# The 0/1 matrix of a token's place is made once per column, and the token's number is multiplied into the narrow matrix

## The chip, the cores and the metric

One core of one Trainium2 chip runs the whole program in one launch. The metric is the device time of that core in microseconds (us), the median of several runs.

## The reference

Attention over pooled keys and values gives 4,608 tokens of 512 numbers. Each goes through one of 8 experts of a first layer, and then, where a skip score is positive, through one of 8 experts of a second one.

```python
def _attn_ref(q, k, v):                       # q, k, v: 8, 8, 576, 64
    k_p = k.reshape(B, H, Sp, pool, D).mean(axis=3)      # pool = 8
    v_p = v.reshape(B, H, Sp, pool, D).mean(axis=3)
    scores = scale * np.matmul(q, k_p.transpose(0, 1, 3, 2))
    ...
    return np.matmul(attn, v_p)

def _moe_ref(x, modality_id, w_gate, modality_bias, w1, w2):
    logits = x @ w_gate + modality_bias[modality_id]
    e_idx = np.argmax(logits, axis=1)
    ...
    for e in range(E):                        # E = 8, w1 512 x 1024, w2 1024 x 512
        mask = e_idx == e
        h = np.maximum(x[mask] @ w1[e], 0.0)
        out[mask] = gate_w[mask, None] * (h @ w2[e])

def _moe2_ref(x, w_skip, w_gate, w1, w2):
    do_compute = x @ w_skip > 0
    ...                                       # the same layer on x[do_compute], without bias
    out[do_compute] = xc + y
```

## The kernel before

**Three stages.** The attention works through 36 columns of 128 tokens. A MoE layer works through blocks of 256 tokens of one expert. In a block `gemm1` (L1300) makes 8 slices of the hidden layer by 12 products of 256 columns each, and `gemm2` (L1314) makes two halves (128 tokens each) of the output by 24 products of 512 columns each; every product stands three times, since numbers are split in a high and a low part. After a slice of `gemm1`, ScalarE makes `hh` (L1303) and VectorE makes `hl` (L1304), which frees the slice's PSUM bank. GpSimd gathers the rows of a block by an indirect DMA (L1245), and TensorE transposes them (L1265, `xT`).

**Where a token goes.** `route` gives for every token its expert, its place within a group of 128 places (`BB`), and which group it is (`RH`). `route_places` (L859) makes for each column of 128 tokens a matrix `OB`: a row for each token, a column for each of the 128 places, a one where the token has that place, times the token's number. The number is held in two parts, `pay`, so that bf16 holds each exactly; so there are two matrices for a column. The narrow matrix `oa` (L960 early, L1096 later) has a one where the token belongs to a group. The product of `OB`, transposed, with `oa`, summed over the columns (L975, L1104), gives for every slot the two parts of its token's number in `W`; `slot_rows` (L992, L994, L997) reads `W` and makes the indices of the gather.

**When.** For the first blocks of either layer, `early_places` and `early_slots` do this for two or four groups, before all tokens are known. For all later blocks `route_slots` does it for 52 groups, in steps of six columns, with the products three steps behind; that happens during block 1 of the layer (`second`, L1563), 36 columns in layer 1 and 52 in layer 2. In layer 2's routing, which runs within the blocks of layer 1, `route_places` makes two columns a block on GpSimd.

**What sets the order.** Nothing is scheduled by a program: instructions stand on each engine in the order in which the code issues them. The side work is written as generators. `bg.tick()`, called at fixed places of the main work, takes the next `bg.pace` steps of the first generator in the queue; `bg.flush()` takes all that are left. So the number of `yield`s decides beside which main work a step stands. In `second`, `tick` is called twice after each slice of `gemm1`, `flush` after the first half of `gemm2`, and then come `gather(2)` and, within the second half of `gemm2`, `xT(2)`.

## Time and profile before

| what | before |
|---|---|
| three runs | 1021.94, 1027.18, 1029.12 us, median 1027.18 |
| span of the profiled execution | 1021.7 us |
| mean granted clock of TensorE | 0.972 |
| TensorE busy | 953.3 us, 93% |
| VectorE busy | 713.9 us, 70% |
| GpSimd busy | 606.4 us, 59% |

The page has no time of the profiled execution beside its span, which runs from the first instruction to the last. It is 0.2 us under the fastest run and 5.5 us under the median. The shares are means over stages of different kinds: attention to about 200 us, block 0 and 1 of layer 1 to 275 us, steady blocks of layer 1 to about 750 us, layer 2 to the end.

### The profile page before, as it was taken

To read this page: it belongs to the slowest core of one execution; us is meant where nothing else is said; L and a number is where in the kernel's file an instruction comes from. 1 tells how busy PE (TensorE), PEld (TensorE's weight loads), DVE (VectorE), ACT (ScalarE), POOL (GpSimd) and SP (SyncE) were. 2 spreads that over 40 slices of the span, in tenths; PEclk is the share of its full clock that TensorE was granted. 3 is DMA by queue.
4 is the path that set the end of the run, shared out by engine and by line. 5 is a ranking of instruction groups with operands and counts; after the bars stand their busy time and mean duration, and the time that the engine had idled before them with its cause. 6 is when DMAs were issued, how large, how long until landed. Compare 5 with 4: busy or idle time off the path is not lost. (4 is left out here: it accounts for less than half of the span.)

```text
span 1021.7 us, 20008 instructions
## 1 busy us (share of the span) xinstructions
PE 953.3 (93%) x6647; PEld 859.1 (84%) x6647; DVE 713.9 (70%) x1683; ACT 526.0 (51%) x1072; POOL 606.4 (59%) x816
## 2 busy tenths in 40 slices
PE   6888879899999999999999999999898999999995
PEld 5787879787788888888888888888786998888995
DVE  6699998886666666666666766667455667667665
ACT  4345545432455555555555655555313556555454
POOL 4675856554577777677777777767544333444442
PEclk8789989998999999999999999999899999999998
DMA  9998864520111111342223511226214662661341
GB/s 226 205 248 245 199 172 156 177 68 9 43 53 68 56 60 57 126 148 69 71 73 118 170 68 62 70 71 206 93 56 132 217 226 83 204 207 33 103 154 31
DMA packets 88353, 123.51 MB, mean 121 GB/s; under 512 B 15615, under 2 KB 52479, under 8 KB 88224
## 3 DMA queue, kind: packets, MB, share of 16 engines
q1 hardware_dynamic: 77904, 94.38, 30.9%
q0 software_dynamic: 10320, 27.59, 8.6%
q8 instruction: 59, 0.97, 0.4%
q14 instruction: 70, 0.57, 0.2%
HBM read 181.29 MB, written 39.48 MB: 216 GB/s over the span
## 5 line engine op out<-in xcount | busy, mean ns | idle before, releaser
L1300 PE MATMUL ps_g<-xh,w1h 128*128 128x256 f32 x992 | 289.2, 291 | 13.2 <-DVE hl L1304 8.0
L1300 PE MATMUL ps_g<-xl,w1h 128*128 128x256 f32 x992 | 280.2, 283 | 0.0
L1300 PE MATMUL ps_g<-xh,w1l 128*128 128x256 f32 x992 | 280.2, 282 | 0.0
L1253 POOL TENSOR_TENSOR w1l<-w1r,w1h 128x512 fp32r<-128x512 f32 x122 | 156.6, 1305 | 150.9 <-ACT w1h L1252 150.1
L1303 ACT ACTIVATE hh<-ps_g 128x256 fp32r<-128x256 f32 x248 | 95.5, 385 | 231.4 <-PE ps_g L1300 225.8
L1300 PEld LDWEIGHTS ps_g<-xh,w1h 128*128 128x128 f32 x992 | 188.2, 190 | 22.1 <-DVE hl L1304 10.5
L1314 PE MATMUL ps_g<-w2h,hh 128*128 128x512 f32 x464 | 190.5, 411 | 0.6 <-DVE rs_v L994 0.5
L1300 PEld LDWEIGHTS ps_g<-xl,w1h 128*128 128x128 f32 x992 | 188.6, 190 | 0.6 <-DVE xl L1269 0.2
L1300 PEld LDWEIGHTS ps_g<-xh,w1l 128*128 128x128 f32 x992 | 188.2, 190 | 0.0
L1314 PE MATMUL ps_g<-w2h,hl 128*128 128x512 f32 x464 | 185.1, 399 | 0.0
L1314 PE MATMUL ps_g<-w2l,hh 128*128 128x512 f32 x464 | 185.0, 399 | 0.0
L1259 DVE TENSOR_TENSOR w2l<-w2r,w2h 128x512 fp32r<-128x512 f32 x227 | 162.9, 719 | 17.7 <-ACT w2h L1258 1.5
L1304 DVE SCALAR_TENSOR_TENSOR hl<-ps_g,hh 128x256 fp32r<-128x256 f32 x248 | 105.0, 423 | 91.4 <-ACT hh L1303 85.9
L1258 ACT CAST w2h<-w2r 128x512 fp32r<-128x512 f32 x232 | 141.8, 612 | 3.0 <-DVE gidxf L997 3.0
L1252 ACT CAST w1h<-w1r 128x512 fp32r<-128x512 f32 x240 | 135.4, 618 | 4.9 <-DMA w1r<-in_moe_w_dram 4.9
L859 POOL TENSOR_SCALAR OB<-iota,BB,pay 128x128 bf16<-128x128 bf16 x126 | 110.8, 888 | 24.7 <-DVE BB L847 24.7
L1314 PEld LDWEIGHTS ps_g<-w2h,hl 128*128 128x128 f32 x464 | 88.3, 190 | 20.8
L1253 DVE TENSOR_TENSOR w1l<-w1r,w1h 128x512 fp32r<-128x512 f32 x118 | 101.2, 880 | 5.6 <-POOL rt_eq L796 5.2
L1314 PEld LDWEIGHTS ps_g<-w2h,hh 128*128 128x128 f32 x464 | 88.5, 191 | 18.1 <-issue 1.5
L1314 PEld LDWEIGHTS ps_g<-w2l,hh 128*128 128x128 f32 x464 | 88.6, 191 | 16.8
L1269 DVE TENSOR_TENSOR xl<-ps_x,xh 128x512 fp32r<-128x512 f32 x64 | 43.8, 686 | 57.3 <-ACT xh L1268 57.3
L1373 ACT ACTIVATE x<-ps_g,gate 128x512 f32<-128x512 f32 x37 | 25.5, 689 | 82.4 <-PE R L831 43.4
(256 smaller groups left out, 1463.9 us busy)
## 6 DMA issues: line engine op xcount, KB each, us to landing
w1r<-in_moe_w_dram SPq DMA_DIRECT2D x128, 512.0 KB
w2r<-in_moe_w_dram SPq DMA_DIRECT2D x128, 512.0 KB
x2s<-x SPq DMA_DIRECT2D x19, 522.0 KB
v<-in_v_dram SPq DMA_DIRECT2D x16, 576.0 KB
xd<-x SPq DMA_DIRECT2D x16, 520.0 KB
q_sb<-in_q_dram SPq DMA_DIRECT2D x16, 512.0 KB
kt<-in_k_dram SPq DMA_DIRECT2D x8, 576.0 KB
x2s<-OBx SPq DMA_DIRECT2D x16, 261.0 KB
```

The source lines that it names most:

```text
L859: e.tensor_scalar(g.ob(c)[:, i, :], g.iota, r.BB[:, c:c + 1], r.pay[:, i, c:c + 1], ALU.is_equal, ALU.mult)
L1252: self.nc.scalar.copy(self.w1h[f], raw)
L1253: (eng or self.nc.vector).tensor_tensor(self.w1l[f], raw, self.w1h[f].bitcast(F32), ALU.subtract)
L1258: self.nc.scalar.copy(self.w2h[f], raw)
L1259: (eng or self.nc.vector).tensor_tensor(self.w2l[f], raw, self.w2h[f].bitcast(F32), ALU.subtract)
L1269: nc.vector.tensor_tensor(self.xl[i % 2][:, :, 128 * t:128 * t + 128], ps, hi.bitcast(F32), ALU.subtract)
L1300: nc.tensor.matmul(ps, lhsT=a[f][:, k, :], rhs=b[:, k, :], start=(n == 0), stop=(n == 11))
L1303: nc.scalar.activation(out=self.hh[f], in_=ps, func=ACTF.Relu)
L1304: nc.vector.scalar_tensor_tensor(self.hl[f], in0=ps, scalar=0.0, in1=self.hh[f].bitcast(F32), op0=ALU.max, op1=ALU.subtract)
L1314: nc.tensor.matmul(ps, lhsT=a[f][:, tt], rhs=b[f], start=(n == 0), stop=(n == 23))
L1373: nc.scalar.activation(out=self.x2[i % 2][:, t, 0:DM], in_=ps, func=ACTF.Copy, scale=self.gate[i % 2][:, t:t + 1])
```

## The change

`OB` gets one matrix per column, ones and zeros alone, and is made by one instruction in place of two. The token's number goes into `oa`: a new function multiplies the 0/1 matrix `eq` of the groups by either part of `pay` and puts the two results side by side, so that one product with twice as many columns takes the place of two. `route_places` now has one step for a column. Where the second engine helps (columns 18 to 26 and 27 to 35), it takes the odd columns. The buffer `OBx`, which `zero` clears, has half the size.

```diff
-    g.OB = [const.tile([128, C1, 2, 128], BF16, name="OB")]
+    g.OB = [const.tile([128, C1, 128], BF16, name="OB")]
...
 def route_places(tc, g, r, c0, n, eng, eng2=None):
     for c in range(c0, c0 + n):
-        for i in range(2):
-            if c > c0:
-                yield
-            e = eng2 if eng2 is not None and i else eng
-            e.tensor_scalar(g.ob(c)[:, i, :], g.iota, r.BB[:, c:c + 1],
-                            r.pay[:, i, c:c + 1], ALU.is_equal, ALU.mult)
+        e = eng2 if eng2 is not None and c % 2 else eng
+        e.tensor_scalar(g.ob(c), g.iota, r.BB[:, c:c + 1], None, ALU.is_equal)
         yield
+
+
+def places_tokens(tc, oa, eq, pay):
+
+    n, w = eq.shape[1], eq.shape[2]
+    for i in range(2):
+        tc.nc.vector.tensor_tensor(oa[:, :, i, :], eq,
+                                   pay[:, i, :].unsqueeze(2).to_broadcast([128, n, w]), ALU.mult)
...
-    oa = r.oa[C] = sp.tile([128, C, n], BF16, tag=f"er_oa{C}", name="er_oa", bufs=1)
-    V.tensor_tensor(oa, g.iota_a[:, j0:j0 + n].unsqueeze(1).to_broadcast([128, C, n]),
+    oa = r.oa[C] = sp.tile([128, C, 2, n], BF16, tag=f"er_oa{C}", name="er_oa", bufs=1)
+    eq = sp.tile([128, C, n], F32, tag=f"er_eq{C}", name="er_eq", bufs=1)
+    V.tensor_tensor(eq, g.iota_a[:, j0:j0 + n].unsqueeze(1).to_broadcast([128, C, n]),
                     a.unsqueeze(2).to_broadcast([128, C, n]), ALU.is_equal)
     yield
+    places_tokens(tc, oa, eq, r.pay[:, :, 0:C])
+    yield
...
     for c in range(C):
-        for i in range(2):
-            nc.tensor.matmul(W[:, i, :], lhsT=g.ob(c)[:, i, :], rhs=oa[:, c, :],
-                             start=(c == 0 and i == 0), stop=(c == C - 1 and i == 1),
-                             skip_group_check=True)
+        nc.tensor.matmul(W.rearrange("p i n -> p (i n)"), lhsT=g.ob(c),
+                         rhs=oa[:, c].rearrange("p i n -> p (i n)"),
+                         start=(c == 0), stop=(c == C - 1))
...
-            oa = sp.tile([128, n, NSLOT], BF16, tag="rs_oa", name="rs_oa", bufs=lag + 1)
-            V.tensor_tensor(oa[:, 0:m, :], g.iota_a.unsqueeze(1).to_broadcast([128, m, NSLOT]),
+            oa = sp.tile([128, n, 2, NSLOT], BF16, tag="rs_oa", name="rs_oa", bufs=lag + 1)
+            eq = sp.tile([128, n, NSLOT], BF16, tag="rs_eq", name="rs_eq", bufs=1)
+            V.tensor_tensor(eq[:, 0:m, :], g.iota_a.unsqueeze(1).to_broadcast([128, m, NSLOT]),
                             a[:, c0:c0 + m].unsqueeze(2).to_broadcast([128, m, NSLOT]),
                             ALU.is_equal)
+            places_tokens(tc, oa[:, 0:m], eq[:, 0:m, :], r.pay[:, :, c0:c0 + m])
             oas.append(oa)
...
-        g.OB.append(p.tile([128, NSLOT - C1, 2, 128], BF16, name="OBx"))
+        g.OB.append(p.tile([128, NSLOT - C1, 128], BF16, name="OBx"))
```

The products of `route_slots` are changed in the same way as those of `early_slots`. Comments are taken out as well, so lines after L859 have other numbers: L960 becomes L965, L1096 L1103, L1300 L1306, L1304 L1310, L1314 L1320.

Since `route_places` has fewer steps, what follows it in the queue comes earlier. The first place is the end of the attention, on VectorE. Before, these rows stand in a line: the group matrix of the early slots, the reading of `W` (L992 to L997), and then, behind three splits of weights, the routing of the last nine columns (L790 to L804):

```order
L960 TENSOR_TENSOR er_oa<-iota_a,er_a 128x54
L1304 SCALAR_TENSOR_TENSOR hl_2452<-ps_g_2808,hh_2451 128x256
L992 COPY rs_lo<-W_2823 128x2
L994 SCALAR_TENSOR_TENSOR rs_v<-W_2823,rs_lo 128x2
L997 TENSOR_SCALAR gidxf_600<-rs_v 128x2
L1259 TENSOR_TENSOR w2l_2909<-w2r_2455,w2h_2908 128x512
L1259 TENSOR_TENSOR w2l_2911<-w2r_2456,w2h_2910 128x512
L1259 TENSOR_TENSOR w2l_2913<-w2r_2456,w2h_2912 128x512
L790 TENSOR_REDUCE rt_mx<-LG 128x9
L792 TENSOR_TENSOR rt_eq<-LG,rt_mx 128x72
L794 TENSOR_SCALAR rt_eq<-rt_eq 128x72
```

Now the early slots are done some twenty rows ahead, and the routing stands among the last slices of `gemm1`; the three splits (L1265 now) come after `M` (L804):

```order
L1310 SCALAR_TENSOR_TENSOR hl_2415<-ps_g_2778,hh_2414 128x256
L794 TENSOR_SCALAR rt_eq<-rt_eq 128x72
L796 TENSOR_TENSOR rt_eq<-rt_eq,desc 128x72
L1310 SCALAR_TENSOR_TENSOR hl_2417<-ps_g_2797,hh_2416 128x256
L800 TENSOR_REDUCE rt_my<-rt_eq 128x9
L1310 SCALAR_TENSOR_TENSOR hl_2419<-ps_g_2816,hh_2418 128x256
L802 TENSOR_TENSOR rt_eq<-rt_eq,rt_my 128x72
L804 TENSOR_SCALAR M_583<-rt_eq 128x72
L1265 TENSOR_TENSOR w2l_2855<-w2r_2422,w2h_2854 128x512
L1265 TENSOR_TENSOR w2l_2857<-w2r_2423,w2h_2856 128x512
L1265 TENSOR_TENSOR w2l_2859<-w2r_2423,w2h_2858 128x512
L811 CAST rt_ms<-M_583 128x72
```

On TensorE the two products that this routing feeds (`R`) stand behind 18 products of block 0's `gemm2` before:

```order
L1314 MATMUL ps_g_2934<-w2h_2908,hh_2447 128x512
L1314 MATMUL ps_g_2934<-w2l_2909,hh_2447 128x512
L1314 MATMUL ps_g_2934<-w2h_2908,hl_2448 128x512
L830 LDWEIGHTS trim
L830 MATMUL R<-M_583,trim 128x72
L831 LDWEIGHTS ones
L831 MATMUL R<-rt_i,ones 128x72
L1314 MATMUL ps_g_2934<-w2h_2910,hh_2449 128x512
```

and behind nine of them now:

```order
L1320 MATMUL ps_g_2880<-w2h_2604,hh_1861 128x512
L1320 MATMUL ps_g_2880<-w2l_2605,hh_1861 128x512
L1320 MATMUL ps_g_2880<-w2h_2604,hl_1862 128x512
L830 LDWEIGHTS trim
L830 MATMUL R<-M_583,trim 128x72
L831 LDWEIGHTS ones
L831 MATMUL R<-rt_i,ones 128x72
L1320 MATMUL ps_g_2880<-w2h_2606,hh_2410 128x512
```

The second place is VectorE in block 1 of layer 2, where the slots of all later blocks are made. Before, one instruction makes the group matrix of six columns between two `hl`:

```order
L1096 TENSOR_TENSOR rs_oa<-iota_a,rs_a 128x312
L1304 SCALAR_TENSOR_TENSOR hl_2450<-ps_g_15297,hh_2449 128x256
L1053 TENSOR_TENSOR rc_le<-rc_on,rc_last 128x216
L1055 TENSOR_REDUCE rc_ch<-rc_le 128x27
L1096 TENSOR_TENSOR rs_oa<-iota_a,rs_a 128x312
L1304 SCALAR_TENSOR_TENSOR hl_2452<-ps_g_15316,hh_2451 128x256
L1057 SCALAR_TENSOR_TENSOR rc_ch<-blk,rc_ch 128x27
```

Now it is three, the second and third in one row with "x2":

```order
L1103 TENSOR_TENSOR rs_eq<-iota_a,rs_a 128x312
L864 TENSOR_TENSOR rs_oa<-rs_eq,pay_617 128x6x52 x2
L1310 SCALAR_TENSOR_TENSOR hl_2417<-ps_g_15110,hh_2416 128x256
L1059 TENSOR_TENSOR rc_le<-rc_on,rc_last 128x216
L1061 TENSOR_REDUCE rc_ch<-rc_le 128x27
L1103 TENSOR_TENSOR rs_eq<-iota_a,rs_a 128x312
L864 TENSOR_TENSOR rs_oa<-rs_eq,pay_617 128x6x52 x2
L1310 SCALAR_TENSOR_TENSOR hl_2419<-ps_g_15132,hh_2418 128x256
```

The place of the first of the three is that of the one before. The third place is the same work in block 1 of layer 1, where two groups stand between two `hl` now, one before. Before:

```order
L1096 TENSOR_TENSOR rs_oa<-iota_a,rs_a 128x312
L1304 SCALAR_TENSOR_TENSOR hl_2446<-ps_g_3178,hh_2445 128x256
L859 TENSOR_SCALAR OB<-iota,BB_585,pay_587 128x128
L1053 TENSOR_TENSOR rc_le<-rc_on,rc_last 128x216
L1055 TENSOR_REDUCE rc_ch<-rc_le 128x27
L1096 TENSOR_TENSOR rs_oa<-iota_a,rs_a 128x312
L1057 SCALAR_TENSOR_TENSOR rc_ch<-blk,rc_ch 128x27
L1304 SCALAR_TENSOR_TENSOR hl_2448<-ps_g_3199,hh_2447 128x256
```

and now:

```order
L1310 SCALAR_TENSOR_TENSOR hl_1858<-ps_g_3023,hh_1857 128x256
L1103 TENSOR_TENSOR rs_eq<-iota_a,rs_a 128x312
L864 TENSOR_TENSOR rs_oa<-rs_eq,pay_587 128x6x52 x2
L1059 TENSOR_TENSOR rc_le<-rc_on,rc_last 128x216
L1061 TENSOR_REDUCE rc_ch<-rc_le 128x27
L1103 TENSOR_TENSOR rs_eq<-iota_a,rs_a 128x312
L864 TENSOR_TENSOR rs_oa<-rs_eq,pay_587 128x6x52 x2
L1063 SCALAR_TENSOR_TENSOR rc_ch<-blk,rc_ch 128x27
L1310 SCALAR_TENSOR_TENSOR hl_1860<-ps_g_3054,hh_1859 128x256
```

The work on the last nine columns' `OB` stands ahead of these rows now, not among them.

## Rows read from the trace of the kernel before

**Rows 1.** The page's first part: of each engine the busy time, its share of the span, and the number of instructions (PE is TensorE, PEld its loading of weights, DVE VectorE, ACT ScalarE, POOL GpSimd).

```profile
PE 953.3 (93%) x6647; PEld 859.1 (84%) x6647; DVE 713.9 (70%) x1683; ACT 526.0 (51%) x1072; POOL 606.4 (59%) x816
```

**Rows 2.** The windows of 25 us: from and to, length, busy time of PE, PEld, DVE, ACT and POOL with instructions in brackets, the granted clock of TensorE, the DMA engines' share, GB/s. In order: attention, block 1 of layer 1, a steady block, block 1 of layer 2.

```profile
100.00:125.00 25.00, 23.01 (x196) 21.95 (x195) 24.61 (x63) 14.06 (x25) 18.75 (x20) 1.00 0.71 181
...
250.00:275.00 25.00, 24.38 (x213) 21.33 (x212) 16.86 (x58) 10.30 (x22) 9.58 (x22) 1.00 0.14 44
325.00:350.00 25.00, 25.00 (x169) 22.54 (x169) 15.93 (x38) 14.42 (x31) 18.24 (x29) 1.00 0.20 69
750.00:775.00 25.00, 24.63 (x245) 21.47 (x244) 16.84 (x67) 5.26 (x12) 8.44 (x10) 1.00 0.12 47
```

**Rows 3.** The instructions of the four lines that the change touches: number, shortest, median and longest duration in ns, first and last start in us, forms.

```profile
L1104 PE MATMUL W<-rs_oa,OB x144: 184/185/200, 257.4 to 771.8; 128*128 128x52 bf16 x144
L975 PE MATMUL W<-er_oa,OB x154: 163/163/178, 178.5 to 678.7; 128*128 128x2 bf16 x90, 128*128 128x4 bf16 x64
L859 POOL TENSOR_SCALAR OB<-iota,BB,pay x126: 783/796/1565, 105.9 to 723.9; 128x128 bf16<-128x128 bf16 x126
L1096 DVE TENSOR_TENSOR rs_oa<-iota_a,rs_a x15: 367/475/523, 254.4 to 772.1; 128x312 bf16<-128x312 f32 x14, 128x208 bf16<-128x208 f32 x1
```

**Rows 4.** The timeline of TensorE at two places where a run of products into `W` is followed by a product of `gemm2`: start in us, duration, line, tiles; "x64" counts the products of a run.

```profile
677.09 1.76 PE L975 MATMUL W<-er_oa,OB 128*128 128x4 bf16 x64
678.95 0.49 PE L1314 MATMUL ps_g<-w2h,hh 128*128 128x512 f32 x1
...
771.80 1.09 PE L1104 MATMUL W<-rs_oa,OBx 128*128 128x52 bf16 x32
772.72 0.48 PE L1314 MATMUL ps_g<-w2h,hh 128*128 128x512 f32 x1
```

**Rows 5.** The timeline of GpSimd and of VectorE late in the attention: `OB` of four columns' halves, the first step of the pooling of keys (L177), and one addition on VectorE (L380) at two times.

```profile
122.05 3.75 POOL L859 TENSOR_SCALAR OB<-iota,BB,pay 128x128 bf16<-128x128 bf16 x4
125.76 2.33 POOL L177 TENSOR_TENSOR t<-kt 108x1024 f32<-108x1024 f32 x1
...
114.68 0.15 DVE L380 TENSOR_TENSOR LG<-ls,BT 128x8 f32<-128x8 f32 x1
...
125.30 2.82 DVE L380 TENSOR_TENSOR LG<-ls,BT 128x8 f32<-128x8 f32 x1
```

**Rows 6.** The timeline of TensorE from the early slots to the first product of block 1 (in brackets: how long the engine stood idle before, and who released it).

```profile
223.83 1.49 PE L975 MATMUL W<-er_oa,OB 128*128 128x2 bf16 x54 [1.18 <-DVE er_oa L960]
225.86 0.47 PE L1314 MATMUL ps_g<-w2h,hh 128*128 128x512 f32 x1 [0.54 <-DVE rs_v L994]
...
233.77 0.22 PE L830 MATMUL R<-M,trim 128*128 128x72 bf16 x1 [1.95 <-DVE M L804]
234.58 0.28 PE L831 MATMUL R<-rt_i,ones 128*128 128x72 bf16 x1 [0.59 <-DVE rt_i L815]
234.61 0.77 PE L1314 MATMUL ps_g<-w2h,hh 128*128 128x512 f32 x1
...
239.87 0.95 PE L1265 MATMUL ps_x<-ident,xg 128*128 128x128 f32 x4
...
242.48 0.48 PE L1314 MATMUL ps_g<-w2h,hh 128*128 128x512 f32 x1
...
245.35 0.28 PE L1300 MATMUL ps_g<-xh,w1h 128*128 128x256 f32 x1
```

**Rows 7.** The timelines of VectorE and of GpSimd there: one comparison of the routing in an earlier round and in the last one, and the clearing of `OBx`.

```profile
181.82 0.20 DVE L794 TENSOR_SCALAR rt_eq<-rt_eq 128x72 f32<-128x72 f32 x1
...
229.03 3.66 DVE L794 TENSOR_SCALAR rt_eq<-rt_eq 128x72 f32<-128x72 f32 x1
...
229.10 3.53 POOL L1223 MEMSET OBx<- 128x4096 bf16 x1
```

**Rows 8.** Block 1 of layer 1 in the timelines of VectorE, TensorE and GpSimd: the first group matrix, the start of `gemm2`, the gather for block 2 and the transposes of its rows.

```profile
254.37 0.48 DVE L1096 TENSOR_TENSOR rs_oa<-iota_a,rs_a 128x312 bf16<-128x312 f32 x1
...
260.85 0.48 PE L1314 MATMUL ps_g<-w2h,hh 128*128 128x512 f32 x1
...
263.12 1.10 POOL L1245 DMA_INDIRECT xg<-xd,gidx  x1 [11.89 <-DVE rs_lo L1113]
...
269.71 0.60 PE L1265 MATMUL ps_x<-ident,xg 128*128 128x128 f32 x4
```

**Rows 9.** Block 1 of layer 2 in the timelines of VectorE and TensorE: the first group matrix and the next row behind it, three rows before which VectorE stood idle, the reading of `W`, the transposes of block 2's rows and the first product of block 2.

```profile
762.98 0.47 DVE L1096 TENSOR_TENSOR rs_oa<-iota_a,rs_a 128x312 bf16<-128x312 f32 x1
763.37 0.41 DVE L1304 SCALAR_TENSOR_TENSOR hl<-ps_g,hh 128x256 fp32r<-128x256 f32 x1
...
769.48 0.48 DVE L1096 TENSOR_TENSOR rs_oa<-iota_a,rs_a 128x312 bf16<-128x312 f32 x1 [0.92 <-PE W L1104]
770.58 0.48 DVE L1096 TENSOR_TENSOR rs_oa<-iota_a,rs_a 128x312 bf16<-128x312 f32 x1 [0.62 <-PE W L1104]
771.37 0.75 DVE L1453 SCALAR_TENSOR_TENSOR o<-ps_g,gate,xg 128x512 f32<-128x512 f32 x1 [0.30 <-PE ps_g L1314]
...
773.86 0.21 DVE L992 COPY rs_lo<-W 128x52 f32<-128x52 f32 x1 [1.39 <-PE W L1104]
...
779.56 0.79 PE L1265 MATMUL ps_x<-ident,xg 128*128 128x128 f32 x4 [3.80 <-DMA xg<-x2s,gidx]
...
784.82 0.28 PE L1300 MATMUL ps_g<-xh,w1h 128*128 128x256 f32 x1
```

More of the change, by code (lines that the diff above doesn't have):

```diff
@@ L968, in early_slots @@
     oa = r.oa.pop(C)
-    n = oa.shape[2]
+    n = oa.shape[3]
     yield
@@ L1102, in route_slots @@
             for c in range(b0, min(b0 + n, C)):
-                for i in range(2):
-                    nc.tensor.matmul(W[:, i, :], lhsT=g.ob(c)[:, i, :],
-                                     rhs=oas[b0 // n][:, c - b0, :],
-                                     start=(c == 0 and i == 0), stop=(c == C - 1 and i == 1),
-                                     skip_group_check=True)
+                nc.tensor.matmul(W.rearrange("p i n -> p (i n)"), lhsT=g.ob(c),
+                                 rhs=oas[b0 // n][:, c - b0].rearrange("p i n -> p (i n)"),
+                                 start=(c == 0), stop=(c == C - 1))
         for _ in range(pace):
@@ L1212, in zero @@
     def zero(self):
-        return self.g.OB[1].rearrange("p c i n -> p (c i n)").bitcast(F32)[:, 0:W2C]
+        return self.g.OB[1].rearrange("p c n -> p (c n)").bitcast(F32)[:, 0:W2C]
     def open_gating(self):
```

## The prediction, made before the changed kernel ran

> **What bounds the kernel now.** I read the page's busy times first: TensorE is busy for 93% of the span, VectorE for 70%, GpSimd for 59% [rows 1]. The windows tell what that mean is made of [rows 2]. In a steady block TensorE is busy for 25.00 of 25 us, and there only fewer or shorter products save time. Late in the attention VectorE is the full one, 24.61 us of 25. In block 1 of either layer TensorE has 24.4 and 24.6 us of 25 and VectorE 16.9, but nearly all that VectorE has there is one chain that the next block waits for. So I went through the places where the change's four lines run [rows 3], in the timelines, and asked at each what stands behind them.
>
> **The products of TensorE.** There were 144 + 32 products of `route_slots` and 154 of `early_slots`; half of them go. The duration of one, 163 to 185 ns [rows 3], is not its price, since they are pipelined: 64 pairs of weight load and product take 678.95 - 677.09 = 1.86 us, 29 ns each, and 32 take 772.72 - 771.80 = 0.92 us, 29 ns too [rows 4]. The early products stay narrow (4 or 8 columns), so each pair left out is worth 29 ns. In layer 1's last block that is 32 x 29 ns = 0.9 us on a full engine; in the attention it is 18 x 29 ns = 0.5 us. The 27 at the transition are counted there. For the slots one product of 104 columns replaces two of 52. Its price lies between 29 ns and what the same columns cost in the widest products, where twelve of 512 columns take 245.35 - 242.48 = 2.87 us [rows 6], 239 ns each or 0.47 ns a column: 49 ns for 104. The two that it replaces take 58. With 49, the value of the nearer row, 88 of them save 0.8 us, with 29 they save 2.6; but as VectorE will set their times (below), I count 0. Together **-1.4 us** (-0.9 to -4.0).
>
> **GpSimd's matrices.** Of 126 instructions of 0.8 us [rows 3] about half go. In layer 1's blocks that is some 28 us less work on GpSimd, but TensorE is full there [rows 2] and waits for none of it: worth 0. If that cover were gone, it would be at most the same 28 us; nothing in the window points to it.
>
> In the attention VectorE is the bound and is held up by GpSimd: the addition L380 takes 0.15 us at 114.68 and 2.82 at 125.30, where it ends with the two GpSimd instructions that ran [rows 5]. Of the 2.67 us lost, 0.5 lie beside `OB` (which ends at 125.80) and the rest beside the pooling of keys. Fewer `OB` move the pooling earlier, so such a stall may vanish or come once more: -2.7 to +2.7; I take the part beside `OB`, **-0.5 us**.
>
> **The transition to the MoE layers.** Before, TensorE loses 1.18 + 0.54 us around the early slots, 1.95 + 0.59 before the two products `R` [rows 6], 4.26 us in all, and after that runs at the lower of its two clock levels: twelve products from 234.61 to 239.87 take 438 ns each, against 239 ns later [rows 6]. The wait for `R` comes from one comparison that takes 3.66 us, 0.20 in an earlier round, while GpSimd clears `OBx` [rows 7]. Now the early slots' products stand among the last products of `gemm1`, with no fresh wait before them, and `gemm2` starts 1.1 to 2.1 us earlier. The routing is earlier too, but `R` stands behind nine products of `gemm2`, not 18, and the three weight splits stand between `M` and the rest of its chain. From the rows' durations (three splits 1.9 us on VectorE, the chain behind them 0.7) `R` would make TensorE wait for 2.1 us, or 3.75 if the clearing, half as long now (1.77 us), still holds a VectorE instruction up. I expect the sum of waits to fall by 0.5 to 2 us and the low stretch to be about as long: by this term alone block 1 starts at 242.7 instead of 245.35, **-2.6 us** (-0.6 to -4.3).
>
> On which instructions the clearing holds, the Trainium skill ("SBUF — State Buffer", section "Who interferes with whom") says that VectorE's two-port modes, as of `tensor_scalar`, lock against any GpSimd instruction, but that an instruction with two inputs in SBUF contends only with a GpSimd instruction that reads. The 3.66 us row is a `tensor_scalar` and agrees. By the page the splits would pass the clearing, and the wait for `R` would be the 2.1 us; by the row alone it could be 3.75. The sum lies between.
>
> **Block 1 of layer 1.** Every group of six columns gets two multiplications more on VectorE. No row shows one. The nearest is the comparison of the same 312 elements: 0.47 us long, with the next instruction 0.39 us after its start [rows 9]. If a multiplication is as long, a group costs 2 x 0.39 us and the wait for the comparison's own result, 0.1 us: 0.89 us, and six groups 5.3 us. From below, an instruction of 72 elements takes 0.20 us [rows 7], so a group could be as cheap as 0.5; from above, 0.5 us for each multiplication gives 6.6 us. Worse, the order puts two groups between two `hl`, where one stood, and `hl` frees the bank that `gemm1` writes to next. So TensorE waits in `gemm1`, by my walk through the new order 0.75 us behind the first slices and 3.75 us behind the later ones. Against that, `OB` of the last nine columns no longer stands in this stretch. `gemm2` starts 15.5 us after `gemm1` before (260.85 - 245.35) [rows 6, 8], and 19.9 to 20.6 now: **+4.6 us** (+3.7 to +6.6, the upper end if the clock falls after the wait). The gather moves with it; it has 6.6 us to the transposes (263.12 to 269.71) [rows 8] and stays hidden.
>
> **Block 1 of layer 2.** Nine groups here: eight full ones at 0.89 us and a last one of four columns at 0.7 us make 7.8 us more on VectorE from 762.98 on [rows 9]. It stood idle there for 0.92 + 0.62 + 0.30 = 1.84 us, and of the 1.39 us before it reads `W` some 0.9 are not needed by the last few products: 7.8 - 1.84 - 0.9 = 5.0 us, up to 6.0 if that 0.9 stays. Behind `W` stand the indices, the gather and the transposes, for which TensorE already waits for 3.80 us [rows 9]: nothing covers the 5 us. TensorE's work after the transposes takes 784.82 - 779.56 = 5.26 us with a first part at the low clock level and would take about 3.7 at the high one; a third of that difference I give back, since waits that TensorE has earlier in the stretch may spare it. **+4.5 us** (+3.4 to +6.0).
>
> **Sum:** -1.4 - 0.5 - 2.6 + 4.6 + 4.5 = +4.6 us on the profiled 1021.7, 1026.3 us. That execution lies at the fast end of the runs and 5.5 us under the median, so on the median of 1027.18 it is **1031.7 us**. This kernel's three runs differ by 7.2 us; about 1%, 10.3 us, is what its measurement can tell from no change.
>
> **Rivals.**
> *Faster.* The stalls of the attention vanish (-2.7), the transition gives its best (-4.3), products count 29 ns everywhere (-4.0), and the multiplications cost the lower 0.2 us, so that the two blocks 1 lose 2 and 2.5 us: -6.5 us, 1020.7. For it: the long rows of VectorE there lie beside GpSimd work that is now halved. Against: each needs its own luck. Chance 0.13.
> *Multiplications hidden.* VectorE has 8 us idle of 25 in both windows of block 1 [rows 2]; if the chain can use that, both blocks cost 1 to 2 us in place of 9, and the time is about -2.5 us, 1024.7. Against: of the idle time, only 1.84 us lie in the chain [rows 9]. Chance 0.10.
> *Slower by over 1%.* The mechanism is the clock: where TensorE has waited in block 1, it comes back at the low level, as at 234.61, where twelve products cost 2.4 us more than at the high one [rows 6]. If both blocks 1 pay that (2 x 2.4 us), and the multiplications take the upper 0.5 us with a wait of their own each (1.3 and 1.7 us more), it is 4.6 + 4.8 + 3.0 = +12.4 us, 1039.6. It decides if the waits in block 1 come in one piece, as the two that ended at 233.77 and 234.58 did (2.5 us together) [rows 6]. Chance 0.15.
> *The change doesn't save what it says.* If half the `OB` work freed nothing and the transition stayed as it is, the sum is +9.1 - 1.4 = +7.7, 1034.9, within the forecast's own range; it is part of it.
>
> **How the numbers follow.** The forecast has 0.62, over +0.5 to +9 us (1027.7 to 1036.2 on the median), and is the likeliest. Faster by over 1% needs more than the whole first rival and then some: 0.05. Slower by over 1% is the third rival with a little of the forecast's upper end: 0.17. Within 1%: 0.78. The range leaves out the far half of the faster rival and of the slower one: 1021 to 1040 us.
>
> **What would show each step.** In the profile after: the early products at about 29 ns a pair, half as many; 0.39 us from one multiplication (L864) to the next row; the wait before `R` at 2 to 4 us, block 1 of layer 1 starting 3.6 us earlier in all than at 245.35 (0.5 + 0.5 + 2.6), with `gemm1` there stalled twice behind `hl`; in layer 2, no idle VectorE between the group matrices and the wait for the gather 4 to 5 us longer. The prediction is wrong if a multiplication costs half or twice that, if TensorE's clock falls at new places, or if the attention's stalls on VectorE move as a whole.

## The result, and the profile after

The changed kernel took 1039.66 us (median of 4 runs, 1035.52 to 1042.03), the kernel before 1027.63 beside it: **slower by 1.09%**, ratio 1.0109 with a 95% interval of 1.0066 to 1.0152. In a second series, which stands among the experiments, it was 1040.29 against 1029.03, ratio 1.0112 (1.0087 to 1.0136). One run of the kernel before in that series and one in that of the last experiment were slow (2916 and 1836 us) and are left out of every median here. The forecast was 1031.7 in a range of 1021 to 1040; the first series lies 0.3 us inside the range, the second 0.3 us outside it, both some 8 us from the forecast. The profiled execution has a span of 1040.3 us, against 1021.7; the 18.6 us between them are more than the change, since this execution was the slowest of its four (1042.03 us) and the one of before lies at the fast end of its own.

The page's busy times, to be held against [rows 1]:

```profile
PE 955.6 (92%) x6482; PEld 862.2 (83%) x6482; DVE 727.7 (70%) x1710; ACT 526.1 (51%) x1072; POOL 540.9 (52%) x751
```

165 TensorE instructions fewer and 66 us less work on GpSimd, as the change says, and 14 us more on VectorE. TensorE is busy for 2.3 us more than before, though it has fewer products: its extra time is waiting, and time at a lower clock.

**Where the time is.** A table from the timelines: how long each stretch took, from the 36 additions of the attention's columns (L380 on VectorE) and the first product of each block. Two profiles of either kernel, the second of each from the experiments; the last column is the difference of the means.

| stretch, us | before | again | after | again | difference |
|---|---|---|---|---|---|
| attention, column 1 to 11 | 55.6 | 63.2 | 65.1 | 60.2 | +3.2 |
| column 11 to 27 | 81.2 | 79.9 | 82.4 | 84.2 | +2.8 |
| column 27 to block 1 of layer 1 | 68.4 | 67.5 | 69.6 | 67.1 | +0.4 |
| of it, block 0 | 44.3 | 43.2 | 44.8 | 42.5 | -0.1 |
| block 1 of layer 1 | 28.9 | 28.9 | 34.6 | 35.7 | **+6.3** |
| blocks 2 to 18 (layer 1's last) | 445.3 | 445.9 | 445.8 | 445.5 | 0.0 |
| block 0 of layer 2 | 32.2 | 31.8 | 28.8 | 28.7 | **-3.3** |
| block 1 of layer 2 | 33.1 | 33.1 | 37.4 | 37.4 | **+4.3** |
| the rest, to the end of the last product | 226.0 | 225.8 | 224.9 | 225.9 | -0.5 |

From column 27 to the end that is +7.3 us, and it repeats. The first 27 columns scatter by more than the change can be told from: in column 1 to 11 no instruction has changed, and the same program took 55.6 and 63.2 us there.

**Block 1 of layer 2**, the clearest place. VectorE (start, duration, line; "x2" counts two multiplications) and TensorE:

```profile
777.83 0.48 DVE L1103 TENSOR_TENSOR rs_eq<-iota_a,rs_a 128x312 bf16<-128x312 f32 x1
778.35 0.88 DVE L864 TENSOR_TENSOR rs_oa<-rs_eq,pay 128x312 bf16<-128x312 bf16 x2
779.15 0.42 DVE L1310 SCALAR_TENSOR_TENSOR hl<-ps_g,hh 128x256 fp32r<-128x256 f32 x1
...
794.39 0.21 DVE L998 COPY rs_lo<-W 128x52 f32<-128x52 f32 x1 [0.59 <-PE W L1111]
...
780.23 0.45 PE L1111 MATMUL W<-rs_oa,OB 128*128 128x104 bf16 x6
...
789.06 0.43 PE L1111 MATMUL W<-rs_oa,OB 128*128 128x104 bf16 x6 [1.06 <-DVE rs_oa L864]
790.57 0.68 PE L1111 MATMUL W<-rs_oa,OBx 128*128 128x104 bf16 x6 [1.07 <-DVE rs_oa L864]
...
800.09 0.63 PE L1271 MATMUL ps_x<-ident,xg 128*128 128x128 f32 x4 [0.50 <-DMA xg<-x2s,gidx]
...
803.95 0.28 PE L1306 MATMUL ps_g<-xh,w1h 128*128 128x256 f32 x1
```

Two multiplications take 779.15 - 778.35 = 0.80 us, 0.40 each. The whole group takes 1.32 us (779.15 - 777.83) where one instruction took 0.39 [rows 9]: 0.93 us more. The three rows before which VectorE waited [rows 9] have no counterpart; now TensorE waits for the group matrix. All such waits, by line:

```profile
L864 DVE TENSOR_TENSOR rs_oa<-rs_eq,pay x30: 369/478/484, 260.3 to 793.4; 128x312 bf16<-128x312 bf16 x28, 128x208 bf16<-128x208 bf16 x2
...
who waited for it (us, times):
  PE W L1111: 9.3, 9
  PE W L981: 3.2, 1
```

`W` is read 27.87 us after the block's first product (766.52), 22.17 before (773.86 - 751.69). Of these 5.7 us the block gets 1.4 back, since TensorE's work from the transposes to the next block takes 3.86 us (803.95 - 800.09) against 5.26 [rows 9]: the wait of 3.80 us for the gather, after which the clock was low, is now 0.50 (1.5 in the second profile).

**Block 1 of layer 1** has the same, from two groups between two `hl`. `gemm2` starts 21.7 us after `gemm1` (279.04 - 257.36), 15.5 before [rows 6, 8]:

```profile
259.74 0.47 DVE L1103 TENSOR_TENSOR rs_eq<-iota_a,rs_a 128x312 bf16<-128x312 f32 x1
260.25 0.88 DVE L864 TENSOR_TENSOR rs_oa<-rs_eq,pay 128x312 bf16<-128x312 bf16 x2
...
263.19 0.43 PE L1111 MATMUL W<-rs_oa,OB 128*128 128x104 bf16 x6 [0.62 <-DVE rs_oa L864]
267.35 0.43 PE L1111 MATMUL W<-rs_oa,OB 128*128 128x104 bf16 x6 [1.29 <-DVE rs_oa L864]
269.73 0.43 PE L1111 MATMUL W<-rs_oa,OB 128*128 128x104 bf16 x6 [1.94 <-DVE rs_oa L864]
...
279.04 0.39 PE L1320 MATMUL ps_g<-w2h,hh 128*128 128x512 f32 x1
```

The rows of `W` show what TensorE waits for: not `hl`, but the group matrices of `W`'s products, which stand among the slices of `gemm1`. There are three such waits, of 0.62, 1.29 and 1.94 us, 3.9 in all, three of 3.9 in the second profile too, and none before. Behind them TensorE's granted clock was 0.50, the lower of its two levels, for 3.4 us (270.7 to 274.1), in the second profile for 6.9 us; products of `gemm1` follow one another there by 0.21 us in place of 0.12.

Both blocks as a whole, layer 1 before and after, then layer 2 before and after (columns as in [rows 2]): VectorE works 2.9 us more in layer 1, where the `OB` of the last nine columns is gone, and 7.7 us more in layer 2, and TensorE's granted clock went from 1.00 to 0.95 and from 0.95 to 0.86.

```profile
245.35:274.22 28.87, 28.25 (x245) 25.20 (x244) 18.90 (x68) 11.44 (x24) 11.43 (x24) 1.00 0.12 39
257.36:291.91 34.55, 30.07 (x209) 26.57 (x208) 21.75 (x68) 11.43 (x24) 8.09 (x20) 0.95 0.09 32
...
751.69:784.82 33.13, 28.96 (x260) 24.91 (x260) 20.60 (x73) 8.07 (x18) 12.51 (x13) 0.95 0.24 80
766.52:803.95 37.43, 31.05 (x209) 25.69 (x208) 28.28 (x91) 8.09 (x18) 10.43 (x11) 0.86 0.21 70
```

**The transition** gains nothing. TensorE, then VectorE and GpSimd:

```profile
228.24 0.82 PE L981 MATMUL W<-er_oa,OB 128*128 128x4 bf16 x27 [3.20 <-DVE er_oa L864]
...
239.38 0.39 PE L1306 MATMUL ps_g<-xh,w1h 128*128 128x256 f32 x1 [1.49 <-DVE hl L1310]
243.35 0.80 PE L1320 MATMUL ps_g<-w2h,hh 128*128 128x512 f32 x1 [2.27 <-DVE hl L1310]
...
247.11 0.21 PE L830 MATMUL R<-M,trim 128*128 128x72 bf16 x1
...
257.36 0.28 PE L1306 MATMUL ps_g<-xh,w1h 128*128 128x256 f32 x1
...
236.06 2.93 DVE L792 TENSOR_TENSOR rt_eq<-LG,rt_mx 128x72 f32<-128x72 f32 x1
...
239.25 2.97 DVE L794 TENSOR_SCALAR rt_eq<-rt_eq 128x72 f32<-128x72 f32 x1
...
236.38 3.80 POOL L1265 TENSOR_TENSOR w2l<-w2r,w2h 128x512 fp32r<-128x512 f32 x3
...
240.36 1.81 POOL L1229 MEMSET OBx<- 128x2048 bf16 x1
```

The four waits of before [rows 6], 4.26 us, are gone, and `R` waits for nothing. In their place are three of 3.20, 1.49 and 2.27 us, 6.96 in all. The early slots stand among the last columns of the attention, where TensorE waits for a group matrix that VectorE has queued behind that column's work. The routing, now among the last `hl`, has two long rows in place of the one of 3.66 us [rows 7], L792 beside GpSimd's weight splits and L794 beside the last of these and the clearing; each holds up the `hl` behind it. `gemm2` starts 30.8 us after block 0's first product (24.9 before), and takes 14.0 us to block 1 (19.5 before).

How long such rows are depends on what they meet. In the second profile of the changed kernel L792 and L794 took 1.34 and 1.14 us, each beside one split of GpSimd, and the waits for `hl` shrank to one of 0.9 us; only the 3.20 us of the early slots stood as before, and block 0 took 42.5 us in place of 44.8. There L804, a `tensor_scalar`, met the clearing, and VectorE's three splits stood right behind it. They took 1.89 us from the first start to the last end, as they do at 243.58 in the first profile with no clearing beside them (last row), and were done 0.4 us after it ended:

```profile
238.03 1.71 DVE L804 TENSOR_SCALAR M<-rt_eq 128x72 bf16<-128x72 f32 x1
238.14 1.89 DVE L1265 TENSOR_TENSOR w2l<-w2r,w2h 128x512 fp32r<-128x512 f32 x3
...
237.88 1.79 POOL L1229 MEMSET OBx<- 128x2048 bf16 x1
...
243.58 1.89 DVE L1265 TENSOR_TENSOR w2l<-w2r,w2h 128x512 fp32r<-128x512 f32 x3
```

**Block 0 of layer 2** (the twentieth block, "block 19" in the expectations) gains 3.3 us, which no term of the sum speaks of. Before, TensorE had two waits that nothing in the trace explains, and the low clock after the second, for 6.8 us; after, it has one, and the low clock for 3.4 us. The first two rows are of the kernel before, the third is of the changed one:

```profile
719.51 0.36 PE L1300 MATMUL ps_g<-xh,w1h 128*128 128x256 f32 x1 [1.80 <-issue]
...
722.50 0.58 PE L1300 MATMUL ps_g<-xh,w1h 128*128 128x256 f32 x1 [2.04 <-issue]
...
737.71 0.36 PE L1306 MATMUL ps_g<-xh,w1h 128*128 128x256 f32 x1 [2.25 <-issue]
```

### The profile page after: what moved, and what is told of

It is laid out like the page before. It is cut to its first block, busy times and chain, and to the rows that moved or that the text cites. A ratio compares the mean times of both kernels' runs of the same rounds, so it can differ in the third digit from the quotient of the medians.

```text
span 1040.3 us, 19644 instructions
## 1 busy us (share of the span) xinstructions
PE 955.6 (92%) x6482; PEld 862.2 (83%) x6482; DVE 727.7 (70%) x1710; ACT 526.1 (51%) x1072; POOL 540.9 (52%) x751
## 5 line engine op out<-in xcount | busy, mean ns | idle before, releaser
L1306 PE MATMUL ps_g<-xh,w1h 128*128 128x256 f32 x992 | 289.6, 292 | 11.5 <-DVE hl L1310 8.1
L1306 PE MATMUL ps_g<-xh,w1l 128*128 128x256 f32 x992 | 281.1, 283 | 0.0
L1306 PE MATMUL ps_g<-xl,w1h 128*128 128x256 f32 x992 | 280.7, 283 | 0.0
L1306 PEld LDWEIGHTS ps_g<-xh,w1h 128*128 128x128 f32 x992 | 188.9, 190 | 19.6 <-DVE hl L1310 10.0
L1320 PE MATMUL ps_g<-w2h,hh 128*128 128x512 f32 x464 | 190.2, 410 | 2.4 <-DVE hl L1310 2.3
L1306 PEld LDWEIGHTS ps_g<-xl,w1h 128*128 128x128 f32 x992 | 189.4, 191 | 0.5 <-DVE xl L1275 0.2
L1306 PEld LDWEIGHTS ps_g<-xh,w1l 128*128 128x128 f32 x992 | 188.9, 190 | 0.0
L1320 PE MATMUL ps_g<-w2l,hh 128*128 128x512 f32 x464 | 184.6, 398 | 0.0
L1320 PE MATMUL ps_g<-w2h,hl 128*128 128x512 f32 x464 | 184.5, 398 | 0.0
L1265 DVE TENSOR_TENSOR w2l<-w2r,w2h 128x512 fp32r<-128x512 f32 x227 | 162.0, 714 | 17.2 <-ACT w2h L1264 0.4
L1310 DVE SCALAR_TENSOR_TENSOR hl<-ps_g,hh 128x256 fp32r<-128x256 f32 x248 | 105.1, 424 | 89.1 <-ACT hh L1309 85.0
L1320 PEld LDWEIGHTS ps_g<-w2h,hl 128*128 128x128 f32 x464 | 88.0, 190 | 20.8
L1320 PEld LDWEIGHTS ps_g<-w2h,hh 128*128 128x128 f32 x464 | 88.3, 190 | 19.2 <-DVE hl L1310 2.5
L1320 PEld LDWEIGHTS ps_g<-w2l,hh 128*128 128x128 f32 x464 | 88.4, 190 | 16.7
L347 PE MATMUL ps_av<-VB,et 96*128 96x146 f32 (+1 forms) x480 | 70.1, 306 | 4.5 <-DVE x L373 4.4
L293 PE MATMUL ps_s<-KB,qt 128*128 128x144 f32 (+1 forms) x320 | 50.6, 314 | 22.7 <-DVE ec L307 17.3
```

The costliest lines, as they stand in the source:

```text
L293: nc.tensor.matmul(ps[p0:p1, hp // 2, (hp % 2) * 144:(hp % 2) * 144 + 144], lhsT=t[:, hp, p0:p1], rhs=KB[b % NR][:, hp, :], start=True, st ...
L347: nc.tensor.matmul(ps[p0:p1, j // 3, o:o + 2 * VW], lhsT=t[:, j, p0:p1], rhs=VB[b % NR][:, j].rearrange("p i w -> p (i w)"), start=(j % 3 ...
L1265: (eng or self.nc.vector).tensor_tensor(self.w2l[f], raw, self.w2h[f].bitcast(F32), ALU.subtract)
L1306: nc.tensor.matmul(ps, lhsT=a[f][:, k, :], rhs=b[:, k, :], start=(n == 0), stop=(n == 11))
L1310: nc.vector.scalar_tensor_tensor(self.hl[f], in0=ps, scalar=0.0, in1=self.hh[f].bitcast(F32), op0=ALU.max, op1=ALU.subtract)
L1320: nc.tensor.matmul(ps, lhsT=a[f][:, tt], rhs=b[f], start=(n == 0), stop=(n == 23))
```

## The experiments

My theory (M): VectorE's multiplications cost the two blocks 1 about 10 us, and the late start of the MoE layers is scatter. The rivals: the attention itself got longer (A), the moved steps are the cost (O), the new addresses are (P).

**Both kernels once more**, for the scatter.

> The changed kernel once more, unchanged. Theory M (multiplications): the change costs about 10 us in block 1 of the two layers (5.7 + 4.3 in the first profile), and the 11.5 us by which block 0 of layer 1 started later in that profile (212.53 against 201.01) is largely scatter of the loads in the attention, since 9.7 us of it were there at the eleventh column, before any changed instruction had run. Then this run's total is 1035 to 1042 us, its block 0 starts anywhere from 200 to 213, and blocks 1 stay at 34.5 and 37.4 us within 0.7. Rival A (attention): the changed kernel's attention is really 10 us longer; then block 0 starts at 212 within 2 us again.

> The kernel before once more, as a measure of the scatter of one kernel. Theory M: block 0 of layer 1 starts at another time than 201.0, by up to 10 us, block 1 of layer 1 takes 28.9 and block 1 of layer 2 33.1 us within 0.7; total 1022 to 1029. Rival A: block 0 starts at 201 within 2 us.

Measured: 1040.29 us (ratio 1.0112) and 1028.16 (0.9990, 0.9970 to 1.0009). Block 0 starts at 208.46 and 206.64 us. Rival A in its plain form falls, since either kernel has starts 4 to 6 us apart. The two blocks 1 come out at 35.71 and 37.41 us, and at 28.86 and 33.14 for the kernel before: layer 2 as expected, layer 1 1.2 us above its first profile. Scatter alone doesn't explain the medians either: their difference is 11 to 12 us, of which 7.3 lie behind column 27. So theory M's reading of the late start as scatter holds only in part.

**The steps of before**, twice.

```diff
     for c in range(c0, c0 + n):
+        if c > c0:
+            yield
+            yield
         e = eng2 if eng2 is not None and c % 2 else eng
```

> The changed kernel with as many steps in route_places as before (25 for nine columns), so that the early slots, the routing of the last columns and the two products R stand where they stood before, with all new instructions kept. Theory M: the stretch from block 0 to block 1 of layer 1 returns to about 44.3 us, block 1 of layer 1 to about 32 (the multiplications, but one group between two hl), block 1 of layer 2 stays at 37.4; total 2 to 4 us under the changed kernel. Rival O (order): the moved steps are the cost, and the total falls by 8 us or more. Rival A: the same as rival O, if the moved steps are what lengthens the attention.

> The changed kernel with the steps of before, once more. Its total was 1037 where that of the kernel which differs from it by nine instructions of layer 2 was 1031.3, 5.7 us less, with 1.6 us of it in the changed place. Theory S (scatter of the attention from one loading of a program to the next): the total comes out at another place, 1030 to 1037, and the first eleven columns take 55 to 67 us. Rival B (the build): the total is 1037 within 1.5 us again, and the eleven columns take 66 us within 2.

Measured: 1036.96 us (ratio 1.0069, 1.0051 to 1.0086) and 1036.54 (1.0062, 1.0042 to 1.0083). Block 0 took 39.7 us in both, 2.8 and 5.1 less than in the two profiles of the changed kernel, so the moved steps cost about 4 us, in the transition, and rival O's 8 is too much. It is also 3.5 and 4.6 less than before the change, and not the 44.3 that I expected; 1.4 of that is the comparison, shorter than in [rows 7] beside the halved clearing, but still long (first row below).

Block 1 of layer 1 took 34.8 us, not 32, and layer 2's block 1 stayed at 37.4. The order isn't free in layer 1: `gemm2` starts 19.0 us after `gemm1` in place of 21.7. But the longest wait for a group matrix, 2.10 us (second row), now stands at the end of `gemm1`, and the granted clock was 0.50 from 269.4 to 276.3: the first products of `gemm2` follow one another by 0.43 us in place of 0.23, and from `gemm2` to the next block it is 15.8 us, not 12.9. So the block is as long by another path, and this run doesn't separate the order from the multiplications; one place with two groups between two `hl` is also left.

```profile
239.61 2.22 DVE L794 TENSOR_SCALAR rt_eq<-rt_eq 128x72 f32<-128x72 f32 x1
...
270.43 0.68 PE L1114 MATMUL W<-rs_oa,OB 128*128 128x104 bf16 x6 [2.10 <-DVE rs_oa L867]
```

**The numbers in bf16**, so that all operands of a multiplication have 16 bits.

```diff
-        r.pay = const.tile([128, 2, C], F32, name=f"pay{n}")
+        r.pay = const.tile([128, 2, C], BF16, name=f"pay{n}")
...
-    eq = sp.tile([128, C, n], F32, tag=f"er_eq{C}", name="er_eq", bufs=1)
+    eq = sp.tile([128, C, n], BF16, tag=f"er_eq{C}", name="er_eq", bufs=1)
```

> The changed kernel with the two parts of the token's number, and the early 0/1 matrix, held in bf16 in place of float32, so that all three tensors of a multiplication have 16 bits. If such a multiplication is twice as fast (0.2 us in place of 0.40 from one to the next), six groups in layer 1 and nine in layer 2 save 2.4 and 3.6 us on VectorE; theory M then expects block 1 at 32 and 34 us and a total 5 to 6 us under the changed kernel. If the speed is set by the repeated operand, each multiplication stays at 0.40 us and the total within 1 us of the changed kernel's.

Measured: the multiplications of this kernel are as long as those above:

```profile
L864 DVE TENSOR_TENSOR rs_oa<-rs_eq,pay x30: 368/479/485, 259.9 to 789.3; 128x312 bf16<-128x312 bf16 x28, 128x208 bf16<-128x208 bf16 x2
```

The two blocks took 34.5 and 37.5 us, unchanged: 16-bit numbers alone don't make the multiplication faster. That the repeated operand is what keeps it at 0.40 us fits the run by a number per partition below, but no run multiplies two matrices without a repeated operand. The total, 1034.43 us, is 5.9 under the changed kernel's on the same chip, more than the 1 us that the second reading allowed, but not at this place. In the profile 3 us are in blocks 2 to 18 (0.3 us in every second block) and in layer 2's block 0, and I don't know why; the profiled execution was the slowest of 12 (1038.22 us), so it can't show where the rest lies.

**The second multiplication on GpSimd**, with the steps of before.

```diff
     for i in range(2):
-        tc.nc.vector.tensor_tensor(oa[:, :, i, :], eq,
+        e = tc.nc.gpsimd if gp and i else tc.nc.vector
+        e.tensor_tensor(oa[:, :, i, :], eq,
...
-            eq = sp.tile([128, n, NSLOT], BF16, tag="rs_eq", name="rs_eq", bufs=1)
+            eq = sp.tile([128, n, NSLOT], BF16, tag="rs_eq", name="rs_eq", bufs=4)
```

The 0/1 matrix gets four buffers, so that VectorE needn't wait for GpSimd to have read it.

> The changed kernel with the steps of before, and with the second of the two multiplications of a group in block 1 of both layers done by GpSimd, which stands idle there. Theory M (VectorE's multiplications are the cost of the two blocks): VectorE loses 0.4 us a group, so block 1 falls from 34.8 to about 32 us in layer 1 and from 37.4 to about 34 in layer 2, and the total by 5 to 6 us under the same kernel with both on VectorE (1037). Rival G: GpSimd is slower than the chain allows (over 1.3 us a group), or holds VectorE up, and both blocks stay within 1 us or get longer.

Measured: block 1 took 33.8 us in layer 1 (1 less) and 38.4 in layer 2 (1 more), so rival G: a row of GpSimd is 1.01 us long where one of VectorE is 0.48, and in layer 2 TensorE waits 4.4 us for it, beside 1.3 for VectorE. In layer 1 the profile puts TensorE's waits, 3.6 us, down to VectorE's small rows, so what ended them there isn't shown.

```profile
L868 POOL TENSOR_TENSOR rs_oa<-rs_eq,pay x15: 550/1007/1012, 252.8 to 778.3; 128x312 bf16<-128x312 bf16 x14, 128x208 bf16<-128x208 bf16 x1
```

The total was 1032.15 us, 4.8 under the same kernel with both on VectorE, which is what I had expected for theory M. But the two ran on different chips, and beside this one the kernel before took 1026.59 us, not 1029.03: the ratio is 1.0065 (1.0041 to 1.0088), within the intervals of 1.0069 and 1.0062. So the total shows no gain that can be told from none, and the stretches say the same.

**Layer 2's second multiplication by a number per partition**, with the steps of before, twice.

```diff
+    if one:
+        tc.nc.vector.tensor_scalar(oa[:, :, 1, :], eq, pay[:, 1, 0:1], None, ALU.mult)
+    for i in range(1 if one else 2):
-    for i in range(2):
```

> The changed kernel with the steps of before. In layer 2 the second part of a token's number is the same in all columns, so its multiplication becomes one by a number per partition, with no repeated operand; layer 1 is as it was. Theory M: if such a multiplication takes 0.15 to 0.2 us, nine groups save 1.8 to 2.3 us, block 1 of layer 2 falls from 37.4 to about 35.3, block 1 of layer 1 stays at 34.8, total 1035. Rival: it takes 0.4 us as well (written in pieces of 52), and nothing changes.

> The changed kernel with the steps of before and layer 2's second multiplication by a number per partition, once more. Its total was 1031.3; the kernel without that multiplication's change gave 1037.0 and 1036.5 in two series, and its attention is the same, instruction by instruction. From column 27 to the end the two differ by 0.6 to 0.9 us. Rival B (the build): what is left, about 4.5 us, belongs to the built program, whatever its attention says, and the total is 1031.3 within 1.5 us again. Theory S (scatter from one series to another): the total moves towards 1036, by 2.5 us or more.

Measured: it takes 0.22 us (774.73 - 774.51), and the block 35.8 and 35.7 us, 1.6 less: nine groups by 0.18. VectorE's multiplications set the length of layer 2's block, nearly one for one.

```profile
774.51 0.30 DVE L867 TENSOR_SCALAR rs_oa<-rs_eq,pay 128x312 bf16<-128x312 bf16 x1
774.73 0.48 DVE L869 TENSOR_TENSOR rs_oa<-rs_eq,pay 128x312 bf16<-128x312 bf16 x1
```

The totals were 1031.29 and 1032.37 us, each within the 1.5 us that rival B (the build) allows, and so were the 1037.0 and 1036.5 of the kernel without this edit. But that can't show it, since the four series ran on different chips. Beside the first two the kernel before took 1026.59 and 1027.05 us, beside the others 1029.03 and 1029.98. Against it the kernels lose 4.7 and 5.3 us (ratios 1.0044 and 1.0053), and 7.9 and 6.6 (1.0069 and 1.0062). So of the 4.9 us between the totals some 2.7 go with the chips. Of the 2.2 that are left 1.4 lie behind column 27 (836.0 and 834.5 us there, against 836.5 and 836.7), where the edit takes its 1.6, and the rest is less than the intervals can tell. So rival B isn't shown by these runs.

**The old addresses**, two profiles.

```diff
-    g.OB = [const.tile([128, C1, 128], BF16, name="OB")]
+    g.OB = [const.tile([128, 2 * C1, 128], BF16, name="OB")[:, 0:C1]]
```

> The changed kernel, with the half-size matrices OB kept in a store as large as before, so that all tiles that are laid out behind them have the addresses that they had before. In six profiles the first eleven columns of the attention, which hold no changed instruction, took 55.6 and 63.1 us with the kernel before and 60.1 to 66.9 with the four changed ones. Theory P (place in memory): the loads of the attention depend on the addresses, and with the old ones the eleven columns take 55 to 63 us and the total falls by some 5 us under the changed kernel's 1040. Theory S (scatter): addresses do nothing; the total stays within 2.5 us of 1040 and the eleven columns take anything from 55 to 67 us.

> The same kernel as the one before it, for a second profile of the attention. Theory P: the first eleven columns take 55 to 63 us again. Theory S: anything from 55 to 67 us.

Measured: 1039.13 and 1038.37 us (ratios 1.0127, 1.0098 to 1.0156, and 1.0118), the first eleven columns 67.2 and 67.1 us. Theory P falls.

**Layer 2's early products twice**, to bring back TensorE's number of instructions ahead of layer 2's block 0.

```diff
-    for c in range(C):
+    for c in [*range(C)] * (2 if C == 32 else 1):
```

> The changed kernel, with the 32 products of layer 2's early slots issued twice in a row (the second set starts the sum anew), so that TensorE has as many instructions there as before. From block 19 to layer 2's block 1 the kernel before took 32.2 and 31.8 us, with a second wait of 2.04 us just after the block's start that nothing in the trace explains and a low clock after it; the changed kernels took 27.6 to 28.8, with one such wait. Theory I (instructions): the wait depends on where the instruction stream stands, and comes back: 31 to 32 us. Rival: it depends on something else; then 28.5 us, and only block 17, in which the products stand, is 0.9 us longer.

Measured: the wait is longer, but stays one, and no second follows; the stretch took 29.7 us, neither 31 nor 28.5.

```profile
738.98 0.55 PE L1306 MATMUL ps_g<-xh,w1h 128*128 128x256 f32 x1 [3.91 <-issue]
```

Theory I falls as it stands. All three profiles with the instructions of before have two such waits (1.80 + 2.04, 1.80 + 2.03, 2.12 + 2.37 us), the ten others of changed kernels have one of 1.95 to 2.47, and this one has one of 3.91. So the wait changes with the instructions that stand ahead of it; why the second one came and went stays open. Block 17, in which the products stand, took 29.1 us as with the changed kernel, but block 18 was 30.2 us long, 1.7 and 2.0 longer. The total, 1045.28 us in two runs, is 15.3 us above the kernel before on the same chip (ratio 1.0139, 1.0096 to 1.0182), where the changed kernel lost 11 to 12: the two intervals overlap.

**The kernel before, with the clearing of OBx moved** behind block 1 of layer 1.

```diff
         nc.gpsimd.memset(self.W9s.bitcast(F32), 0.0)
-        nc.gpsimd.memset(g.OB[1], 0.0)
...
         if d:
             d.pop(9)()
+            m.nc.gpsimd.memset(g.OB[1], 0.0)
```

> The kernel before, with one thing moved: the clearing of OBx stands on GpSimd after block 1 of layer 1, not in the middle of block 0. With the changed kernel's matrices and the old steps the stretch from block 0 to block 1 took 39.7 us against 43.2 and 44.3 before. Theory C (clearing): it was the comparison of 3.66 us beside the clearing that this stretch lost; then it takes 40 to 41 us here too, all else is as before, and the total falls by 3 us, to about 1024. Rival W (work): the gain came from half the products and matrices; then the stretch stays at 43 to 44 us.

Measured: **1024.60 us against 1029.98, ratio 0.9931 (0.9905 to 0.9958)**, faster than both kernels. Block 0 took 38.2 us in place of 43.2 and 44.3, with the old products and matrices, so rival W falls; all stretches behind it are as before. The comparison is short again, and the wait of 1.95 us ahead of `R` [rows 6] is gone:

```profile
236.03 0.21 DVE L794 TENSOR_SCALAR rt_eq<-rt_eq 128x72 f32<-128x72 f32 x1
...
237.33 0.19 PE L830 MATMUL R<-M,trim 128*128 128x72 bf16 x1
238.14 0.29 PE L831 MATMUL R<-rt_i,ones 128*128 128x72 bf16 x1 [0.62 <-DVE rt_i L815]
...
284.27 3.51 POOL L1605 MEMSET OBx<- 128x4096 bf16 x1
```

The gain is larger than the 3.45 us by which the comparison got shorter. From `gemm2`'s start to block 1 it is 13.4 us, not 19.5 and 18.4: behind the long wait TensorE ran the rows from 234.61 to 239.87 at the low clock [rows 6]; here the granted clock was 1.00 in all of block 0, 0.88 before. An earlier low stretch of before, 226.9 to 230.3, is gone too, which the clearing at 229.10 doesn't explain.

## Why the prediction was right or wrong

**The early and the wide products: right in the rows.** 32 early products and the first of `gemm2` start 695.01 and 696.07 us, 1.06 us apart, where 64 took 1.86 [rows 4]: 0.8 us saved, 0.9 said. They stand in the last block of layer 1 but one, which took 29.1 us in both profiles, against 28.9 and 29.1 before: in the block the saving doesn't show.

```profile
695.01 0.94 PE L981 MATMUL W<-er_oa,OB 128*128 128x8 bf16 x32
696.07 0.50 PE L1320 MATMUL ps_g<-w2h,hh 128*128 128x512 f32 x1
```

Six wide ones take 0.45 us (the row at 780.23 above), one alone 0.21: (0.45 - 0.21) / 5 = 48 ns from one to the next, 49 said. As VectorE sets their times, nothing of it shows.

**GpSimd's matrices: right for the blocks.** 66 us less work there, and blocks 2 to 18 are 0.0 us shorter. The 0.5 us for the attention is taken up below.

**The transition: wrong**, -2.6 said, +0.4 measured from column 27 on. The step that failed is "with no fresh wait before them": the early slots' products wait for 3.20 us in both profiles. A second one is that the routing's chain, moved in among the `hl`, would only be late for `R`; `R` waits for nothing or 0.5 us (2 to 4 said), but the chain held up `hl` itself, twice by some 2.7 us in one profile and by about 1 us in the other. The run with the old steps shows what the move costs (about 4 us). The row on which I built the term, the 3.66 us comparison, was read rightly: the run with the clearing moved gains by it. On what holds what up: L792 has two inputs in SBUF and was long beside GpSimd's weight splits, which read; L794, a `tensor_scalar`, was long beside the last of these and the clearing. That agrees with the rule of the Trainium skill that the prediction weighed ("SBUF — State Buffer", section "Who interferes with whom"). The second profile also shows the case that the prediction left between 2.1 and 3.75 us: VectorE's splits pass the clearing (1.89 us with it and without), the `tensor_scalar` ahead of them doesn't (1.71 us, 0.20 without).

**Block 1 of layer 1: right on who sets it, wrong on the wait, and too small.** +4.6 said, +5.7 and +6.8 measured. A multiplication costs 0.40 us (0.39 said), a group 0.93 (0.89 said). But I had TensorE wait in `gemm1` for banks that `hl` frees, twice, 4.5 us in all; it waits for the group matrices, three times, 3.9 us. To the start of `gemm2` it is 6.2 and 7.3 us more in place of 4.4 to 5.1. What the sum lacked there is the clock, which I had only in the upper end of the range: 3.4 and 6.9 us at half speed cost at most 1.7 and 3.4 us, an estimate from these lengths.

**Block 1 of layer 2: right, with two errors that cancel.** +4.5 said, +4.3 measured. `W` is read 5.7 us later (5.0 said, up to 6.0), and 1.4 us come back behind the transposes (0.5 said). I had said that the wait for the gather gets 4 to 5 us longer; it fell from 3.80 to 0.50 and 1.5 us, as TensorE now waits earlier, six times and 5.5 us in all, for the group matrices.

**What the sum lacked.** The sum gives 1031.8, where I wrote 1031.7. Block 0 of layer 2, -3.3 us, is in no term; nothing in the rows of before told me that the two unexplained waits change with the instructions ahead of them. And the time ahead of column 27: by the profiles +6.0 us, by the medians 11 to 12 less 7.3, some 4 to 5. I said -0.5 for the attention. In eleven profiles of the changed kernels column 1 to 11 took 60.0 to 67.2 us; in three with the instructions of before 55.6, 63.2 and 65.8. The 27th column's addition starts at 176.9, 182.3 and 183.6 us with the instructions of before, and at 181.0 to 189.1, in the mean 186.0, with the changed ones. Neither the changed instructions (none stands in columns 1 to 11) nor the addresses explain it. It stays open, and with it a third of the measured difference.

**The rivals.** "Slower by over 1%", given 0.17, said 1039.6 us, and the time is there; "within 1%", given 0.78, missed it by little, since the ratios are 1.0109 and 1.0112. The rival's mechanism brought part of the time: the clock did fall in both blocks 1, for 3.4 to 6.9 us in layer 1 and for 10.2 and 6.8 in layer 2, where it was 3.4 before. But layer 2's block cost less than the forecast had it, not more, and the multiplications took 0.40 us, not the upper 0.5. Of the 12 us the two blocks have 10.6, the transition 0.4; block 0 of layer 2 takes 3.3 off, and 4 to 5 are the open part. That the sum of these falls on the rival's number is luck, and so is the edge of the range, 0.3 us to either side. By the prediction's own sign, a clock that falls at new places, it was wrong. "Multiplications hidden" falls by TensorE's 9.3 us of waits for them.

## What to carry to other kernels

Work that is moved from an idle engine to one that stands in a chain costs nearly its full length once the chain's own idle time is used up, however idle that engine is on average: in layer 2 VectorE got 7.7 us more, the block 4.3, and taking 0.18 us from each of nine groups gave 1.6 back. When generators share ticks, removing a step moves everything behind it; here it cost about 4 us, as much as that stretch gained otherwise. A long row of a small instruction (3.66 us for what takes 0.2) can be worth more than a count of instructions: moving the GpSimd instruction beside it gained 0.7% (0.4 to 1.0).
